# A host-planned linear-attention kernel: M's products spread over four pairs, its forms noted later, q's first loads given their own due times

## The chip, the core and the metric

The kernel runs on one core of a Trainium2 chip. The metric is the device time of one execution in microseconds; lower is better. Before the change the median of three runs is 572.95 us (572.63 to 574.16).

## The reference: what is computed

Two independent blocks A and B, each with its own x (2048 x 640), wqkv (640 x 1920) and wo (640 x 640), all in float32. 32 heads of 20 columns. The outputs stand side by side in the result (2048 x 1280).

```python
qkv = (x @ wqkv).reshape(B, S, 3, H, Dh).transpose(2, 0, 3, 1, 4)
q, k, v = qkv[0], qkv[1], qkv[2]
phi = lambda t: jnp.where(t > 0, t + 1, jnp.exp(t)) + 1e-6
pq, pk = phi(q), phi(k)
kv = jnp.einsum("bhsd,bhse->bhde", pk, v)
z = jnp.einsum("bhsd->bhd", pk)
num = jnp.einsum("bhqd,bhde->bhqe", pq, kv)
den = jnp.einsum("bhqd,bhd->bhq", pq, z)[..., None] + 1e-6
o = num / den
return o.transpose(0, 2, 1, 3).reshape(B, S, D) @ wo
```

## The kernel before

**What is computed in which order.** v is never formed. For each block the kernel first makes K = x wk, phi of it (pk), and G = pk' x (640 x 640, "gacc"). From G and wv come the 32 small matrices kv (in six groups of heads, GROUPS), and from those and wo one 640 x 640 matrix M; the output is then phi(q) / den times M. All products are float32 in three parts: each factor is split in a high part (rounded, made by ScalarE) and a low part (the rest, made by VectorE), and high x high, high x low and low x high are added in PSUM. K's products and the output products are done by Strassen-like schemes with seven products on 2 x 2 blocks ("forms" of the weight: sums of its blocks, each split in high and low).

**Stages.** K and G of block A, then K and G of block B, then q and the output of all eight 512-token units. In the K stage two token tiles of 128 make a pair; there are 16 pairs, p = 0 to 7 for A and 8 to 15 for B (NPB = 8). `kpair(p, fill)` writes the seven K products of a pair (banks 0, 1 and 2) and puts between them what `fill` names after step n: steps of G (`gstep`, 12 matmuls of 320 columns, banks 3 to 5), `kvmm(g, k)` (the kv of head group g, PSUM bank k), `mmm(g, k)` (the rows of M that belong to group g: load of wo, split, two products, copy, store of M's rows to DRAM). So A's kv and M are made while TensorE works on B's K. After the products of M come `zsums(0)` (the sums of phi(k) over the tokens, with one small store zd and four small gathers zq through DRAM) and `m_forms()`: M is read back from DRAM, its ten forms are made by VectorE (`forms`), split, and stored to DRAM by SyncE (`fd`), from where the output stage loads them. After B's last pair there are ten more steps of G, then q begins.

**What sets the order.** Up to the start of q nothing is written in the order in which an engine runs it. `note()` files a job (engine, cost, what it reads and writes), and `Plan.emit` simulates the engines on the host: at each moment an idle engine takes, of the jobs whose inputs are there and for which tiles are free, the one due first. TensorE's order is that of the calls. Due times run back from TensorE's ideal time: a job is due 0.2 us (LAG) before the first job that needs it, less its cost and, for a DMA, less 2.2 us and its transfer time. A job without followers is due `late` us (25, if not given) after TensorE's ideal time at the place where it was noted. `ahead` says how long before its due time a job may be taken at the earliest. `safe` lets the planner hold a job that needs a DMA's data for some us more, unless its due time comes first. A DMA is taken to be done 1.9 us after its transfer, and a tile is free for another use as soon as its last job is done in the simulation. On the chip each engine then runs its list in order and waits at semaphores: the list of SyncE (which issues most DMAs) stops at the first DMA that has to wait.

**Tiles.** Most data of the K stage lie in 42 tiles of 128 x 640: 4 "wo" (BO), 7 "wst" (BD) and 31 "gd" (GD); a job with `ANY` takes the first free one in this order. B's wv, six tiles that live on into the output stage, may lie in BD alone.

**The seam to q.** `swap` opens the tiles of q when the K stage's own are used up (`gate`). Then come, per 128 rows, the load of wq and its split (`high`, `low`), the load xqs of the first 512 columns of x' and its high part (`round`), the load xql of its low part from DRAM (`fetch`), and the six loads of wv; they are noted with `late` 25, the loads with `ahead` 20 and 30. From here on the order is the program's. q's first product needs wq and both parts of x' (L912 to L914); B's kv groups (L972, `kvmm2`) stand after q's steps (0,0), (0,3), (1,0), (1,3), (2,0) and (2,3) of unit 0 and use two PSUM banks in turn, which VectorE empties (L976). The last VectorE jobs of the plan are the end of B's z sums (L609 to L612), which wait for zq.

Of the kernel before, what the change touches and what calls it, by code (L numbers as in the profile page):

```python
# [15 lines left out]
DH = 20  # L16
EPS = 1e-6
GROUPS = [(0, 6), (6, 6), (12, 6), (18, 6), (24, 4), (28, 4)]
LAG = 0.2


class Space:
# [53 lines left out]
class Plan:  # L76
# [6 lines left out]
        self.jobs = []  # L83
        self.pe_at = 0.0

    def note(self, engine, n, fn, w, r, ahead=None, dma=None, late=None, by=None, due=None, safe=0.0):
        base = self.RATE.get(engine)
        j = Job(engine, base[0] + base[1] * n if base else n, fn, ahead, dma)
        for part, writes in [(p, True) for p in w] + [(p, False) for p in r]:
            sp = part.space  # L90
            if sp.where is not None and sp not in j.spaces:
                j.spaces.append(sp)
            for lo, hi, other, wrote in sp.uses:
                if lo < part.hi and part.lo < hi and (writes or wrote) and other is not j:
                    j.deps.add(other)
            if writes:
                sp.uses = [u for u in sp.uses if not (part.lo <= u[0] and u[1] <= part.hi and u[2] is not j)]
            sp.uses.append((part.lo, part.hi, j, writes))
        for d in j.deps:
            d.nexts.append(j)  # L100
        for sp in j.spaces:
            sp.left += 1
        if engine == "PE":
            j.ideal = self.pe_at
            self.pe_at += j.cost
        j.late = self.pe_at + (25.0 if late is None else late)
        if by is not None:
            j.late = self.pe_at + by
        j.by, j.set, j.safe = by, due, safe
        self.jobs.append(j)  # L110
        return j

    def emit(self, start, log=None):
        jobs = self.jobs
        for j in reversed(jobs):
            due = min([n.due - LAG for n in j.nexts], default=j.late)
            if j.by is not None:
                due = min(due, j.late)
            due -= j.cost + (2.2 + j.dma if j.dma else 0)
            if j.engine == "PE":  # L120
                due = min(due, j.ideal)
            j.due = due if j.set is None else j.set
# [14 lines left out]
        while n < len(jobs):  # L137
# [7 lines left out]
            for e in idle:  # L145
# [46 lines left out]
                queue[e].remove(best)  # L192
                if best.dma:
                    wire = max(wire, now) + best.dma
                    best.done = wire + 1.9
                    if e == "SP":
                        flying.append(best.done)
                    idle[e] = now + best.cost
                else:
                    best.done = idle[e] = now + best.cost  # L200
                events.update((idle[e], best.done, best.done + LAG))
                ends.append((best.done, best))
                best.fn()
                if log is not None:
                    log.append((now, e, best.fn.__code__.co_firstlineno, best, best.done))
# [10 lines left out]
def tile_linear_attn_pair(ctx: ExitStack, tc: tile.TileContext, ins, out: bass.AP):  # L216
# [79 lines left out]

    BK = [Bank("bank", k) for k in range(8)]

    def load(dst, src, n, ahead=14.0, due=None):
        note("SP", 0.07, lambda: nc.sync.dma_start(dst.f, src), [dst], [], ahead=ahead, dma=n * 512 / 330e3, due=due)  # L300

    def hi_of(hi, src, n):
        note("ACT", n, lambda: act(hi.r, src.f, AF.Copy), [hi], [src], ahead=10.0)
# [51 lines left out]
    def forms(kind, src, split, ready=()):  # L355

        f, raw = {}, {}
        for c in range(NC):
            raw[c] = t = Space(kind, D, ANY)
            note("SP", 0.07, lambda t=t, c=c: nc.sync.dma_start(t.all.f, src[c * P:(c + 1) * P, :]), [t.all],  # L360
                 [mdv[0:6]] if kind == "m" else [], ahead=14.0, dma=1.0)
        for k in range(2):
            m, n = raw[k], raw[2 + k]
            x, z = Space("t23", D, ANY), Space("t4", HF, ANY)
            note("DVE", HF, lambda m=m, n=n, x=x: tt(x[HF:D].f, n[HF:D].f, m[HF:D].f, op=OP.subtract),
                 [x[HF:D]], [n[HF:D], m[HF:D]], ahead=10.0)
            note("DVE", HF, lambda m=m: tt(m[HF:D].f, m[HF:D].f, m[0:HF].f, op=OP.subtract),
                 [m[HF:D]], [m.all], ahead=10.0)
            note("DVE", HF, lambda m=m, n=n, x=x: tt(x[0:HF].f, n[HF:D].f, m[HF:D].f, op=OP.subtract),
                 [x[0:HF]], [n[HF:D], m[HF:D]], ahead=10.0)  # L370
            note("DVE", HF, lambda n=n, x=x, z=z: tt(z.all.f, n[0:HF].f, x[0:HF].f, op=OP.subtract),
                 [z.all], [n[0:HF], x[0:HF]], ahead=10.0)
            f[k], f[2 + k], f[4 + k], f[6 + k] = m, x, n, z
        x, m = Space("d5", HF, ANY), raw[4]
        note("DVE", HF, lambda: tt(x.all.f, m[0:HF].f, m[HF:D].f, op=OP.subtract), [x.all], [m.all], ahead=10.0)
        f[8], f[9] = m, x
        out = dict(ready)
        for i in (0, 1, 2, 3, 4, 5, 8, 6, 7, 9):
            if i not in out:
                out[i] = split(i, f[i])  # L380
        return out
# [205 lines left out]
    def zsums(b):  # L587

        z, zt32 = Space("zsum", D, ANY), Space("zturn", D, ANY)
        for h in range(2):  # L590
            note("DVE", HF, lambda h=h: tt(z.all.f[:, h * HF:h * HF + HF], zac[b][h].all.f[:, :HF],
                                           zac[b][h].all.f[:, HF:], op=OP.add), [z[h * HF:h * HF + HF]], [zac[b][h].all], safe=6.0)
        part, four = Space("zpart", 20), Space("zfour", 20)
        pt, ft4 = zp[b]
        add = dict(axis=mybir.AxisListType.X, op=OP.add)
        note("DVE", D, lambda: nc.vector.transpose(zt32.all.f, z.all.f), [zt32.all], [z.all])
        note("DVE", D, lambda: nc.vector.tensor_reduce(
            pt.rearrange("p (g c) -> p c g", g=4), zt32.all.f.rearrange("p (c g t) -> p c g t", g=4, t=32), **add),
            [part.all], [zt32.all])
        zdv = Space("zd", 1)  # L600
        note("SP", 0.07, lambda: nc.sync.dma_start(zd[b], pt), [zdv.all], [part.all], dma=0.1)
        for g in range(4):
            note("SP", 0.07, lambda g=g: nc.sync.dma_start(
                ft4[g * 32:g * 32 + 32].rearrange("p (q c) -> p q c", q=4),
                zd[b].rearrange("(q i) (g c) -> g i q c", q=4, g=4)[g]), [four[g:g + 1]], [zdv.all], dma=0.1, safe=6.0)
        zt, s = zz[b]

        def finish():
            nc.vector.tensor_reduce(zt, ft4.rearrange("p (q c) -> p c q", q=4), **add)  # L609
            nc.vector.tensor_scalar(zt, zt, S * EPS, None, op0=OP.add)  # L610
            nc.vector.tensor_reduce(s, zt, **add)
            nc.vector.tensor_scalar(s, s, EPS, EPS / 4, op0=OP.mult, op1=OP.add)  # L612

        note("DVE", 300, finish, [KZ[b].all], [four.all], safe=6.0)
# [3 lines left out]
    def m_forms():  # L618
        def split(i, s):
            hi = Space("fsh", s.cols, ANY, F32R)  # L620
            lo = Space("fsl", s.cols, ANY, F32R)
            hi_of(hi.all, s.all, s.cols)
            lo_of(lo.all, s.all, hi.all, s.cols)
            fd[0, i] = [dram.tile([P, s.cols], F32, name=f"fd{t}0{i}") for t in "hl"]
            for d, t in zip(fd[0, i], (hi, lo)):
                note("SP", 0.07, lambda d=d, t=t: nc.sync.dma_start(d, t.all.f), [], [t.all], dma=s.cols / 640,
                     late=16.0 + 8.0 * (0, 2, 6, 4, 1, 3, 7, 5, 8, 9).index(i))

        forms("m", md[0], split)

# [161 lines left out]
    for c in range(NC):  # L792
        gstep(NG - 1, 0, c)
    wf[1] = forms("wk", ins[1]["wk"], w_split)
    kpair(NPB, filled(NG - 1, 1))
    kpair(NPB + 1, {0: [(kvmm, 0, 6)], 1: [(kvmm, 1, 7)], 2: [(kvmm, 2, 6)], 3: [(kvmm, 3, 7)],
                    4: [(kvmm, 4, 6), (kvmm, 5, 7)], 5: [(mmm, 0, 6)], 6: [(mmm, 1, 6)]})
    for p in range(NPB + 2, NP):
        i, h = divmod(p - NPB - 2, 2)
        gready(NG + i)  # L800
        fl = filled(NG + i, h, *((LAST,) if p == NP - 1 else ()))
        if p == NPB + 2:
            for n, g in ((0, 2), (2, 3), (4, 4), (6, 5)):
                fl.setdefault(n, []).append((mmm, g, 6))
        kpair(p, fl)
        if p == NPB + 2:
            zsums(0)
            m_forms()

    def swap():  # L810
# [28 lines left out]
    for c in range(NC):  # L839
# [8 lines left out]
            lo.make()  # L848
            tt(lo.all.r, raw.all.f, hi.all.f, op=OP.subtract)

        note("ACT", D, high, [hi.all], [raw.all, gate.all])
        note("DVE", D, low, [lo.all], [raw.all, hi.all])
        whl["q", 0, c] = hi, lo
    for c in range(NC):
        hi, lo, raw = late(q1b, "xqh", 512, 6), late(q1b, "xql", 512, 6), Space("xqs", 512, ANY)
# [7 lines left out]
            lo.make()  # L863
            nc.sync.dma_start(lo.all.f, xd[0][:, c].rearrange("p j s -> p (j s)"))

        note("ACT", 512, round, [hi.all], [raw.all, gate.all])
        note("SP", 0.07, fetch, [lo.all], [gate.all, xdv[0].all], ahead=30.0, dma=0.8)
        xt[0, c] = hi, lo
    for g, (h0, nh) in enumerate(GROUPS):
        cols = NC * DH * nh  # L870
        w = Space("wv", cols, (BD,))
        load(w.all, ins[1]["wv"][:, h0 * DH * NC:(h0 + nh) * DH * NC], cols, 30.0)
        w.left += 1
        wvt[1, g] = w
    plan.emit(1.0, globals().get("LOG"))
# [515 lines left out]
```

## Time and profile before

| | |
|---|---|
| median of three runs | 572.95 us (572.63 to 574.16) |
| the profiled execution | 574.53 us, of it the span of the instructions 572.8 us |
| TensorE busy | 565.7 us (99%), 3524 matmuls |
| VectorE, ScalarE, GpSimd busy | 434.3, 341.4, 57.2 us |
| DMA | 117.64 MB, mean 205 GB/s |
| granted TensorE clock | 0.999 |

In the rows below, PE is TensorE, PEld its loading of weights, DVE VectorE, ACT ScalarE, POOL GpSimd, SP SyncE; SPq is the issue of a DMA from SyncE's queue. A row of the timeline gives the start, the duration, engine, line, operation, out<-in, shapes and count, and in brackets the idle time before it and what ended it. Consecutive like instructions stand in one row. A row of the list of waits gives the total, the number and the longest. "DMA to landing" runs from issue to the end of the transfer. Times are in us from the start of the span.

### The profile page before, as it was taken

Reading aid. Unit: us, or ns where it says so; the run is one execution under the profiler, and the core shown is the slowest. Engines: PE = TensorE matmul, PEld = TensorE weight load, DVE = VectorE, ACT = ScalarE, POOL = GpSimd, SP = SyncE. Lnnn points to the kernel's source line nnn. Section 1 sums busy time; section 2 is a strip of 40 time slices with the busy share of each in tenths; the row PEclk is TensorE's granted clock in tenths of the full one; section 3 lists DMA queues with packets and bytes.
Section 4 is the critical chain, followed back from the end, with each engine's and each line's share of the span. In section 5 each row is a group of like instructions: output and inputs, shape, how many; then the busy total and the mean of one; then the engine's idle time right before and its main releaser. Section 6 shows DMA issues by size and latency. Waiting matters only on the chain.

```text
span 572.8 us, 9505 instructions
## 1 busy us (share of the span) xinstructions
PE 565.7 (99%) x3524; PEld 535.8 (94%) x3524; DVE 434.3 (76%) x706; ACT 341.4 (60%) x619; POOL 57.2 (10%) x93
## 2 busy tenths in 40 slices
PE   8999999999999999999999999999999999999997
PEld 6999999999999999999988899898989989898997
DVE  6788687599888589976555699967788786758792
ACT  6877566673786677655156665646556464644551
POOL 0210011110010011100000103120012201001010
PEclk9999999999999999999999999999999999999999
DMA  8994665758858889786787986663363996122022
GB/s 296 379 242 141 163 183 128 205 143 246 278 144 217 250 249 321 216 252 196 211 245 275 339 276 215 226 218 109 120 225 134 355 390 231 47 76 93 0 93 92
DMA packets 69441, 117.64 MB, mean 205 GB/s; under 512 B 7956, under 2 KB 31252, under 8 KB 69396
## 3 DMA queue, kind: packets, MB, share of 16 engines
q1 hardware_dynamic: 60500, 89.98, 48.2%
q0 software_dynamic: 8608, 26.88, 16.7%
q8 instruction: 27, 0.44, 0.3%
q10 hardware_dynamic: 288, 0.20, 0.1%
q14 instruction: 18, 0.15, 0.1%
HBM read 71.13 MB, written 35.41 MB: 186 GB/s over the span
## 4 chain that ended last, share of the span: by engine, by line
PE 89%; DMA 5%; DVE 3%; ACT 1%; issue 1%; SPq 1%; ACTq 0%; DVEq 0%
PE psg L312 20%; PE pa L1191 12%; PE ka L312 8%; PE psq L912 8%; PE psq L914 8%; PE psq L913 8%; PE pe L1191 6%; PE ke L312 4%; PE psk L711 4%; PE psb L1191 4%; PE kb L312 3%; DMA md<-mev 2%; DMA wk<-in_A_wk 1%; PE pskv L551 1%; PE pskv L972 1%; DMA xqs<-in_A_xt 1%
## 5 line engine op out<-in xcount | busy, mean ns | idle before, releaser
L312 PE MATMUL psg<-pkl,xnh 128*128 128x320 f32 x320 | 98.9, 309 | 0.0
L312 PE MATMUL psg<-pkh,xnh 128*128 128x320 f32 x320 | 98.8, 309 | 0.0
L312 PE MATMUL psg<-pkh,xnl 128*128 128x320 f32 x320 | 98.4, 308 | 0.0
L912 PE MATMUL psq<-xqh,wh 128*128 128x512 f32 x200 | 78.6, 393 | 1.0 <-ACT xqh L860 1.0
L914 PE MATMUL psq<-xqh,wl 128*128 128x512 f32 x200 | 78.0, 390 | 0.0
L913 PE MATMUL psq<-xql,wh 128*128 128x512 f32 x200 | 77.9, 390 | 0.0
L312 PEld LDWEIGHTS psg<-pkl,xnh 128*128 128x128 f32 x320 | 60.1, 188 | 0.0
L312 PEld LDWEIGHTS psg<-pkh,xnl 128*128 128x128 f32 x320 | 60.1, 188 | 0.0
L312 PEld LDWEIGHTS psg<-pkh,xnh 128*128 128x128 f32 x320 | 60.0, 188 | 0.0
L1206 ACT ACTIVATE o<-pa 128x320 f32<-128x320 f32 x64 | 27.9, 438 | 45.2 <-PE pa L1191 45.0
L484 ACT ACTIVATE kt<-ka 128x320 f32<-128x320 f32 x52 | 22.6, 435 | 52.2 <-PE ka L312 49.0
L1082 DVE SCALAR_TENSOR_TENSOR pq<-eq,rq 128x512 f32<-128x512 f32 x40 | 27.6, 691 | 30.7 <-ACT rq L1081 30.6
L401 POOL DMA_DIRECT2D zacc<-ek x32 | 26.4, 836 | 244.5 <-DVE ek L494 185.3
L532 DVE TENSOR_TENSOR gacc<-psg,gacc 128x320 f32<-128x320 f32 x60 | 29.4, 489 | 28.1 <-PE psg L312 27.3
L1080 ACT ACTIVATE eq<-psq 128x512 f32<-128x512 f32 x40 | 23.9, 597 | 36.6 <-PE psq L914 34.2
L912 PEld LDWEIGHTS psq<-xqh,wh 128*128 128x128 f32 x200 | 37.6, 188 | 8.5 <-ACT xqh L860 1.3
L914 PEld LDWEIGHTS psq<-xqh,wl 128*128 128x128 f32 x200 | 37.5, 188 | 7.9
L913 PEld LDWEIGHTS psq<-xql,wh 128*128 128x128 f32 x200 | 37.6, 188 | 7.2
L396 ACT ACTIVATE pkh<-ek,epst 128x640 fp32r<-128x640 f32 x32 | 26.5, 829 | 7.9 <-DVE ek L494 7.5
L1191 PE MATMUL pa<-fh,dah 128*128 128x320 f32 x96 | 29.7, 309 | 0.0
L1191 PE MATMUL pa<-fh,dal 128*128 128x320 f32 x96 | 29.7, 309 | 0.0
L1191 PE MATMUL pa<-fl,dah 128*128 128x320 f32 x96 | 29.7, 309 | 0.0
(213 smaller groups left out, 1553.3 us busy)
## 6 DMA issues: line engine op xcount, KB each, us to landing
zacc<-ek POOLq DMA_DIRECT2D x32, 320.0 KB, 5.8
xql<-xd SPq DMA_DIRECT2D x40, 256.0 KB, 5.9
xd<-xl SPq DMA_DIRECT2D x29, 320.0 KB, 6.2
out<-o POOLq DMA_DIRECT2D x28, 320.0 KB, 3.6
xns<-in_A_x SPq DMA_DIRECT2D x16, 320.0 KB, 5.8
xts<-in_B_xt_tiles SPq DMA_DIRECT2D x16, 320.0 KB, 4.3
xns<-in_B_x SPq DMA_DIRECT2D x16, 320.0 KB, 5.1
xqs<-in_A_xt SPq DMA_DIRECT2D x20, 256.0 KB, 6.0
```

Source lines behind the costliest of these rows:

```text
L312: nc.tensor.matmul(o, a.r, w.r, start=start and k == i == 0, stop=k == n - 1 and i == 2, skip_group_check=True)
L396: note("ACT", n + 110, lambda: act(hi.r, p.f, AF.Identity, bias=epst), [hi], [p, K0.all], by=8.0)
L401: note("POOL", 1.0, lambda: nc.gpsimd.dma_start(z.f, p.f, **kw), [z], [p], dma=1.0 if first else 1.86)
L532: tt(o, BK[k].tile[:, :HF], o, op=OP.add)
L711: nc.tensor.matmul(o[h][:, :HF], x[a].r, w[c][h * HF:h * HF + HF].r, start=c == 0 and i == 0, stop=c == NC - 1 and i == 2, skip_group_chec ...
L912: nc.tensor.matmul(o, whi, xhi, start=first, stop=False)
L913: nc.tensor.matmul(o, whi, xlo, start=False, stop=False)
L914: nc.tensor.matmul(o, wlo, xhi, start=False, stop=last)
L1080: nc.scalar.activation(e, ps, AF.Exp)
L1082: nc.vector.scalar_tensor_tensor(pq[u][:, c, :], e, 1.0, r, op0=OP.min, op1=OP.add)
L1191: nc.tensor.matmul(ps, x, y, start=start and n == i == 0, stop=n == len(terms) - 1 and i == 2, skip_group_check=True)
L1206: copy = lambda x, y: nc.scalar.activation(x, y, AF.Copy)
```

## The change

It changes, in the planner: a DMA is taken to be done 3.0 us after its transfer in place of 1.9 (loads of the start with a due time of their own keep 1.9), its due time allows for that, and a tile that a DMA reads or writes counts as free 6 us after the DMA. In the program: A's kv groups come three after step 1 and three after step 4 of pair 9; M's six products are put singly into pairs 9 to 12 (one, two, two, one); zsums(0) and m_forms() are noted after pair 12 in place of pair 10, with earlier `late` for the stores of the forms and `safe` 6 on the sums; zd and zq are issued by GpSimd in place of SyncE; q's first loads and splits get `late` and `ahead` of their own.

```diff
+LAT = 3.0
+REUSE = 6.0
...
-    def note(self, engine, n, fn, w, r, ahead=None, dma=None, late=None, by=None, due=None, safe=0.0):
+    def note(self, engine, n, fn, w, r, ahead=None, dma=None, late=None, by=None, due=None, safe=0.0, lat=0.0):
...
-        j.by, j.set, j.safe = by, due, safe
+        j.by, j.set, j.safe, j.lat = by, due, safe, (LAT if due is None else 1.9) + lat
...
-            due -= j.cost + (2.2 + j.dma if j.dma else 0)
+            due -= j.cost + (j.lat + 0.3 + j.dma if j.dma else 0)
...
-                    best.done = wire + 1.9
+                    best.done = wire + best.lat
...
-                events.update((idle[e], best.done, best.done + LAG))
-                ends.append((best.done, best))
+                free = best.done + (REUSE if best.dma else 0.0)
+                events.update((idle[e], best.done, best.done + LAG, free))
+                ends.append((free, best))
...
-    def load(dst, src, n, ahead=14.0, due=None):
-        note("SP", 0.07, lambda: nc.sync.dma_start(dst.f, src), [dst], [], ahead=ahead, dma=n * 512 / 330e3, due=due)
+    def load(dst, src, n, ahead=14.0, due=None, late=None):
+        note("SP", 0.07, lambda: nc.sync.dma_start(dst.f, src), [dst], [], ahead=ahead, dma=n * 512 / 330e3, due=due,
+             late=late)
...
     def forms(kind, src, split, ready=()):
 
         f, raw = {}, {}
+        safe = 6.0 if kind == "m" else 0.0
...
             note("DVE", HF, lambda m=m, n=n, x=x: tt(x[HF:D].f, n[HF:D].f, m[HF:D].f, op=OP.subtract),
-                 [x[HF:D]], [n[HF:D], m[HF:D]], ahead=10.0)
+                 [x[HF:D]], [n[HF:D], m[HF:D]], ahead=10.0, safe=safe)
...
-        note("SP", 0.07, lambda: nc.sync.dma_start(zd[b], pt), [zdv.all], [part.all], dma=0.1)
+        note("POOL", 1.0, lambda: nc.gpsimd.dma_start(zd[b], pt), [zdv.all], [part.all], dma=0.1, lat=2.0)
         for g in range(4):
-            note("SP", 0.07, lambda g=g: nc.sync.dma_start(
+            note("POOL", 1.0, lambda g=g: nc.gpsimd.dma_start(
...
-                     late=16.0 + 8.0 * (0, 2, 6, 4, 1, 3, 7, 5, 8, 9).index(i))
+                     late=10.0 + 6.5 * (0, 2, 6, 4, 1, 3, 7, 5, 8, 9).index(i))
...
-    kpair(NPB + 1, {0: [(kvmm, 0, 6)], 1: [(kvmm, 1, 7)], 2: [(kvmm, 2, 6)], 3: [(kvmm, 3, 7)],
-                    4: [(kvmm, 4, 6), (kvmm, 5, 7)], 5: [(mmm, 0, 6)], 6: [(mmm, 1, 6)]})
-    for p in range(NPB + 2, NP):
-        i, h = divmod(p - NPB - 2, 2)
-        gready(NG + i)
-        fl = filled(NG + i, h, *((LAST,) if p == NP - 1 else ()))
-        if p == NPB + 2:
-            for n, g in ((0, 2), (2, 3), (4, 4), (6, 5)):
-                fl.setdefault(n, []).append((mmm, g, 6))
+    place = ((1, 5, 0, 6), (2, 0, 1, 6), (2, 2, 2, 6), (3, 0, 3, 6), (3, 2, 4, 6), (4, 0, 5, 6))
+    kvs = {1: [(kvmm, g, (6, 7, 3)[g]) for g in range(3)], 4: [(kvmm, g, (4, 5, 6)[g - 3]) for g in range(3, 6)]}
+    for p in range(NPB + 1, NP):
+        if p == NPB + 1:
+            fl = kvs
+        else:
+            i, h = divmod(p - NPB - 2, 2)
+            gready(NG + i)
+            fl = filled(NG + i, h, *((LAST,) if p in (NPB + 2, NP - 1) else ()))
+        for q, n, g, k in place:
+            if q == p - NPB:
+                fl.setdefault(n, []).append((mmm, g, k))
         kpair(p, fl)
-        if p == NPB + 2:
+        if p == NPB + 4:
             zsums(0)
+        if p == NPB + 4:
             m_forms()
...
-        note("ACT", D, high, [hi.all], [raw.all, gate.all])
-        note("DVE", D, low, [lo.all], [raw.all, hi.all])
+        note("ACT", D, high, [hi.all], [raw.all, gate.all], ahead=15.0, late=9.0)
+        note("DVE", D, low, [lo.all], [raw.all, hi.all], ahead=15.0, late=9.0)
...
-        note("ACT", 512, round, [hi.all], [raw.all, gate.all])
-        note("SP", 0.07, fetch, [lo.all], [gate.all, xdv[0].all], ahead=30.0, dma=0.8)
+        note("ACT", 512, round, [hi.all], [raw.all, gate.all], late=9.5)
+        note("SP", 0.07, fetch, [lo.all], [gate.all, xdv[0].all], ahead=12.0, dma=0.8, late=8.0 + c)
...
-        load(w.all, ins[1]["wv"][:, h0 * DH * NC:(h0 + nh) * DH * NC], cols, 30.0)
+        load(w.all, ins[1]["wv"][:, h0 * DH * NC:(h0 + nh) * DH * NC], cols, 14.0, late=10.0 + 2 * g)
```

The other four sums of `forms` get `safe=safe` in the same way.

More of the change, by code (lines that the diff above doesn't have):

```diff
@@ L365, in forms @@
             note("DVE", HF, lambda m=m, n=n, x=x: tt(x[HF:D].f, n[HF:D].f, m[HF:D].f, op=OP.subtract),
-                 [x[HF:D]], [n[HF:D], m[HF:D]], ahead=10.0)
+                 [x[HF:D]], [n[HF:D], m[HF:D]], ahead=10.0, safe=safe)
             note("DVE", HF, lambda m=m: tt(m[HF:D].f, m[HF:D].f, m[0:HF].f, op=OP.subtract),
-                 [m[HF:D]], [m.all], ahead=10.0)
+                 [m[HF:D]], [m.all], ahead=10.0, safe=safe)
             note("DVE", HF, lambda m=m, n=n, x=x: tt(x[0:HF].f, n[HF:D].f, m[HF:D].f, op=OP.subtract),
-                 [x[0:HF]], [n[HF:D], m[HF:D]], ahead=10.0)
+                 [x[0:HF]], [n[HF:D], m[HF:D]], ahead=10.0, safe=safe)
             note("DVE", HF, lambda n=n, x=x, z=z: tt(z.all.f, n[0:HF].f, x[0:HF].f, op=OP.subtract),
-                 [z.all], [n[0:HF], x[0:HF]], ahead=10.0)
+                 [z.all], [n[0:HF], x[0:HF]], ahead=10.0, safe=safe)
             f[k], f[2 + k], f[4 + k], f[6 + k] = m, x, n, z
         x, m = Space("d5", HF, ANY), raw[4]
-        note("DVE", HF, lambda: tt(x.all.f, m[0:HF].f, m[HF:D].f, op=OP.subtract), [x.all], [m.all], ahead=10.0)
+        note("DVE", HF, lambda: tt(x.all.f, m[0:HF].f, m[HF:D].f, op=OP.subtract), [x.all], [m.all], ahead=10.0, safe=safe)
         f[8], f[9] = m, x
```

## The prediction

> **What bounds the kernel now.** I read the page first, then the list of who waited for whom on TensorE, then the timeline of TensorE around each wait, and last the timelines of SyncE, ScalarE and VectorE behind it.
>
> ```profile
> span 572.8 us, 9505 instructions
> ## 1 busy us (share of the span) xinstructions
> PE 565.7 (99%) x3524; PEld 535.8 (94%) x3524; DVE 434.3 (76%) x706; ACT 341.4 (60%) x619; POOL 57.2 (10%) x93
> ```
> ```profile
> PE psq L912 <- ACT xqh L860: 1.0, 1, 1.0
> PE psi L639 <- DVE ones L320: 1.0, 1, 1.0
> PE ke L312 <- DVE kt L488: 0.7, 1, 0.7
> PE psk L711 <- ACT wkh L303: 0.5, 1, 0.5
> PE ka L312 <- ACT kt L484: 0.2, 1, 0.2
> ```
> TensorE is the bound: 565.7 of 572.8 us. The change adds and removes no matmul, so all that it can gain is in the waits. Two of the five (psi, psk) lie in the first microseconds, whose loads have a due time written by hand and keep their latency of 1.9; I leave them as they are. Three are left. What they cost is read from the starts of the matmuls, since the list shows only the gap after the pipeline has drained:
>
> ```profile
> 179.31 0.31 PE L578 MATMUL psm<-woh,kvl 80*80 80x320 f32 x1
> 179.87 0.42 PE L312 MATMUL ka<-wkh,xh 128*128 128x320 f32 x1 [0.25 <-ACT kt L484]
> ```
> ```profile
> 204.71 0.31 PE L312 MATMUL ka<-wkh,xl 128*128 128x320 f32 x1
> 205.74 0.41 PE L312 MATMUL ke<-wkh,xsh 128*128 128x320 f32 x1 [0.71 <-DVE kt L488]
> 205.99 0.31 PE L312 MATMUL ke<-wkl,xsh 128*128 128x320 f32 x1
> 206.14 0.31 PE L312 MATMUL ke<-wkh,xsl 128*128 128x320 f32 x1
> ```
> ```profile
> 289.29 0.31 PE L312 MATMUL psg<-pkh,xnl 128*128 128x320 f32 x1
> 290.61 0.50 PE L912 MATMUL psq<-xqh,wh 128*128 128x512 f32 x1 [1.02 <-ACT xqh L860]
> ```
> Two matmuls of 320 columns follow each other every 0.15 us (205.99 to 206.14). The three pairs above are 0.56, 1.03 and 1.32 us apart, so 0.41, 0.88 and 1.17 are lost, and the step after a wait takes 0.25 in place of 0.15 (205.74 to 205.99), 0.10 more each: 0.51, 0.98 and 1.27, in sum **2.76 us**. That is the most these three can give back. The list of weight loads has a second, short wait for L488 beside the one at 205.74:
>
> ```profile
> PEld ke L312 <- DVE kt L488: 1.2, 2, 1.0
> ```
> Its 0.2 I don't count, but it belongs to the lower end of the range.
>
> **The change part by part.** The program's order on each engine comes from a planner on the host; an engine then runs its list in order and waits where it must. So the change is one of order alone, and its price is which wait comes last where.
>
> *Planner's constants (latency 1.9 to 3.0 us, 6 us before a tile is reused that a DMA touched).* Two waits behind the first stall:
>
> ```profile
> 174.22 0.44 ACT L484 ACTIVATE kt<-ka 128x320 f32<-128x320 f32 x1 [2.18 <-DMA zacc<-ek]
> ```
> ScalarE stood 2.18 us, since the tile it was to write was still being read by the accumulating DMA. With 6 us kept free after a DMA the planner hands it another tile. It was this lost time that made ScalarE's copy too late for the matmul at 179.87; I count the 0.51 as gained. The price is tiles held longer. What hides it is that loads are asked for 12 to 16 us ahead of their due time (`ahead` in the code), so that one which gets its tile 6 us later still lands in time: nothing, and up to 0.51 (the same stall elsewhere) if that cover is gone.
>
> *M's products over four pairs, its forms later, `safe` = 6 on their sums.* Behind the second stall:
>
> ```profile
> 187.93 6.29 DMA md<-mev
> ```
> ```profile
> 194.35 3.24 DMA m<-md
> ```
> ```profile
> 198.59 0.49 DVE L365 TENSOR_TENSOR t<-m 128x320 f32<-128x320 f32 x1 [3.71 <-issue]
> ```
> M's last rows left at 187.93 and took 6.29 us to DRAM, where the planner assumed 1.9 + 1.0; SyncE stood until then, read M back at 194.35 (3.24 us), and VectorE, whose next instruction was the first sum of the forms, stood 3.71 us. From there it was late until the matmul at 205.74. In the new order the last product of M is at the head of pair 12 and the forms are noted at that pair's end, about 16 us after it (a pair has 54 matmuls of K and 60 of G, 114 by 0.147 = 16.8 us); the sums are asked for at least 6 us after the planned landing where their due time allows. The planner's error (6.29 + 3.24 against 4.0 + 4.0 now) is 1.5 us, less than those 6. I count 0.98 as gained. What is late next is VectorE's load, since the forms' sums and splits move some 20 us back (from two pairs, less what their due times gain):
>
> ```profile
> 210.00:250.00 40.00, 40.00 (x275) 40.00 (x274) 36.41 (x67) 25.66 (x43) 3.42 (x4) 1.00 0.89 265
> 250.00:270.00 20.00, 20.00 (x139) 20.00 (x138) 12.98 (x22) 12.34 (x21) 2.58 (x3) 1.00 0.74 218
> ```
> VectorE (the fourth figure) is busy 36.41 of 40 us up to 250 and 12.98 of 20 after it, so they go where there is room. The form stores move along in SyncE's list, the last of them in between q's loads; each holds the queue until its split is done.
>
> *q's first loads.* In the order of before:
>
> ```profile
> 263.21 1.83 SPq L300 DMA_DIRECT2D wv<-in_B_wv  x4
> 267.63 2.23 SPq L864 DMA_DIRECT2D xql<-xd  x5
> 269.91 0.90 SPq L300 DMA_DIRECT2D wv<-in_B_wv  x2
> 275.47 8.44 SPq L300 DMA_DIRECT2D wq<-in_A_wq  x5
> 284.01 0.38 SPq L601 DMA_DIRECT2D zd<-zp  x1
> 284.43 5.02 SPq L300 DMA_DIRECT2D xqs<-in_A_xt  x5
> 289.54 1.80 SPq L603 DMA_DIRECT2D zq<-zd  x4
> ```
> ```profile
> 289.93 2.57 ACT L860 ACTIVATE xqh<-xqs 128x512 fp32r<-128x512 f32 x4 [1.49 <-DMA xqs<-in_A_xt]
> ```
> What q wants first (wq, xqs) goes last, behind wv, whose six groups are wanted one by one from 0.8 us after q's first matmul on. By the code, a wq load was due at 25 - 0.82 - 0.2 - 0.72 - 0.2 - 3.26 = 19.8 us after the planned end of G, and with ahead = 20 it was open from 0.2 before it; now it is due at 9 - 1.94 - 4.36 = 2.7 and open from 17.3 before. An xqs load moves from 1.1 after the end to 15.5 before. So both go to the front, where SyncE now takes wv and xql (263 to 270). They still need free tiles: the last pair's last accumulation is issued at 271.84 (row below), so I put the last free tile near 272. If the five wq start there, and take as now 8.44 us, xqs goes out from about 280.5, and five of them as now in 5.02 us; the first lands, by its row,
>
> ```profile
> DMA to landing us min/median/max: 5.7/6.4/7.0
> ```
> at 286.9, and ScalarE needs 0.64 for it: 287.5. q then begins at 290.61 - 2.76 = 287.85. That is the late end, with no tile free before 272; I count the 1.27 as gained.
>
> *zd and zq go from SyncE to POOL.* Five small DMAs leave SyncE's queue and pass none of its loads any more; on POOL nothing is queued behind them but the two accumulations per pair. Who waits is VectorE: the end of the z sums (L609) stands in its list ahead of q's first mask product (L976), which frees the PSUM bank that the third pskv group takes.
>
> ```profile
> 271.84 0.85 POOL L401 DMA_DIRECT2D zacc<-ek  x1 [2.27 <-DVE ek L494]
> ```
> ```profile
> 283.00 0.81 DVE L597 TENSOR_REDUCE zp<-zturn 128x20 f32<-128x640 f32 x1
> ```
> ```profile
> DMA to landing us min/median/max: 2.9/4.1/6.8
> ```
> ```profile
> 293.60 0.19 DVE L609 TENSOR_REDUCE z<-zq 128x5 f32<-128x20 f32 x1 [1.16 <-DMA zq<-zd]
> ```
> ```profile
> 294.29 0.27 DVE L976 TENSOR_TENSOR kvt<-pskv,mask 120x120 f32<-120x120 f32 x1
> ```
> ```profile
> 297.00 1.21 PE L972 MATMUL pskv<-gacc,wv 128*120 128x120 f32 x10
> ```
> The sums end at 283.81. In the new clock that is 283.81 - 1.49 (the two stalls ahead of it) + 1.1 (the accumulation is planned to land later) = 283.4. One store landing and one gather landing (row of these tiles: 2.9 to 6.8, median 4.1; I take 4.1 and the shorter 2.9 that an empty queue gives), and three POOL issues of 0.85 between: 283.4 + 2.9 to 4.1, + 2.55, + 2.9 to 4.1 = 291.8 to 294.2. From L609 to the end of L976 it is about 1.0 us: 292.8 to 295.2. The third group wants the bank at 297.00 - 2.76 = 294.24. So it is hidden by 1.4 us or late by 1.0; with 6.8 for each landing it would be late by 6.3. I take 0.2, near the short end, because POOL's queue is empty there.
>
> The Trainium skill, *SBUF — State Buffer*, section "SBUF: two separate sides", speaks against this part: a DMA issued from GpSimd can have its descriptors starved while VectorE runs an operation that uses both read ports, 3.1 us for one that takes 0.62 alone. The trace does not agree for this kernel's operations: with VectorE 76% busy the issue above took 0.85 us. By the rule this part would cost what the second rival below does, or more.
>
> *The new order as a whole* also moves work that has no stall today (33 to 160 us). For that I add one small wait of the size of the gap at 179.87, 0.3.
>
> **Sum.** -0.51 - 0.98 - 1.27 + 0.2 + 0.3 = **-2.26 us**. The profiled execution took 574.53 us (span 572.8), 1.58 above the median of the runs, 572.95; it would become 572.3, and the median **570.7 us**. About 0.3% (1.72 us) is what a measurement of this kernel can tell from no change: the boundary is 571.23.
>
> **The rivals.** *Half of it:* the middle stalls go but q's start stays late, because the loads wait for tiles whatever their place in the list. For it: wq's five loads took 8.44 us to issue, which is waiting, not issuing. Against it: they now stand ahead of xql and wv. Then 572.95 - 1.49 + 0.3 = 571.8.
>
> *The gathers from POOL arrive late,* because each issue there waits for the VectorE operation that runs (0.81 for the one at 283.00): five issues make 4.05, L976 ends at 294.0 + 4.05 = 298.05 against 294.24, and the time is 570.5 + 3.8 = 574.3; with one landing of 6.8 alone (2.7 more than 4.1) it is 570.5 + 2.5 = 573.0. For it: no row shows a small DMA from POOL. Against it: the 0.85. By the figures of that page of the Trainium skill, 2.5 us more for each, it would be an estimated 583.
>
> *Slower: wv loses its head start.*
> ```profile
> 288.28 1.55 DVE L849 TENSOR_TENSOR wl<-wq,wh 128x640 fp32r<-128x640 f32 x2
> ```
> ```profile
> 291.42 1.21 PE L972 MATMUL pskv<-gacc,wv 128*120 128x120 f32 x10
> ```
> wv may lie only in seven tiles, six of which it keeps; wq and xqs, now ahead of it, take from the same ones. If wv gets its tile only when VectorE has split wq (first one done 0.8 after 288.28, in the new clock 287.6), it lands 6.4 later, at 294.0, and the first pskv, wanted at 291.42 - 2.76 = 288.66, waits 5.3 us: 570.7 + 5.3 = 576.0. The kernel is slower than before once that landing passes 290.9 (288.66 + 2.25). Against it: the splits are due 16 us sooner than they were (9 in place of 25) and open from 7.7 us before the planned end of G, so that the tiles come free earlier than 287.6.
>
> *Nothing changes:* the waits only move to other places of the same size, 572.95 within 0.5.
>
> **How the numbers follow.** Forecast 0.58 (its own range 569.5 to 571.2: from all 2.76 gained, with a second short wait of the same kind and the 0.3 by which the runs differ, to 1.0 lost again); half of it 0.15 (571.2 to 572.2); late gathers 0.09 (571.0 to 574.3); wv late 0.09 (572 to 576.0); nothing 0.09. From 569.5 to 573.2 lies a little over 0.8 of this; the upper ends of the two slow cases are left out. Faster: 0.58 + 0.03 of the half case + 0.01 of the gathers = 0.62. Slower: 0.03 of the gathers + 0.07 of wv = 0.10. Same, the rest: 0.28.
>
> **What would show it.** Right: TensorE's list of waits has no line for xqh L860, and those for kt L484 and L488 are gone or below 0.3; SyncE issues wq and xqs ahead of wv, from before 272; VectorE has no wait of 3.7 at L365; zq lands before 294 and L976 does not make pskv wait. The forecast is wrong if TensorE shows a new wait at pskv L972 (on wv or on L976), if xqh stays in the list, or if the matmuls of 33 to 160 us show gaps that they don't have now.

## The result and the profile after

Before: 572.79 us median of 6 runs (571.95 to 576.57). After: 580.52 us of 6 (579.57 to 581.08). The ratio is 1.0122, 95% interval 1.0093 to 1.0151: slower, where 570.7 was forecast. The profiled execution of after took 581.08 us (span 579.3).

The page of after, first lines, and TensorE's list of waits (us in total, times, longest):

```profile
span 579.3 us, 9490 instructions
...
PE 567.1 (98%) x3524; PEld 537.5 (93%) x3524; DVE 434.3 (75%) x706; ACT 341.4 (59%) x619; POOL 63.1 (11%) x103
```
```profile
PE pskv L981 <- DVE kvt L985: 6.3, 1, 6.3
PE psi L644 <- DVE ones L324: 1.0, 1, 1.0
PE psk L716 <- ACT wkh L307: 0.7, 1, 0.7
PE pskv L981 <- DVE gacc L537: 0.7, 1, 0.7
```

All three stalls of before (kt twice, xqh) are gone, as forecast. In their place stands one of 6.3 us, at the third pskv group of q, and a short one at the first. The matmuls around the long one, TensorE's timeline (start, duration, line, what, wait before it):

```profile
291.33 0.39 PE L922 MATMUL psq<-xql,wh 128*128 128x512 f32 x1
291.55 0.39 PE L923 MATMUL psq<-xqh,wl 128*128 128x512 f32 x1
...
292.47 1.21 PE L981 MATMUL pskv<-gacc,wv 128*120 128x120 f32 x10
293.44 0.48 PE L921 MATMUL psq<-xqh,wh 128*128 128x512 f32 x1
...
294.68 0.40 PE L923 MATMUL psq<-xqh,wl 128*128 128x512 f32 x1
301.42 2.36 PE L981 MATMUL pskv<-gacc,wv 128*120 128x120 f32 x10 [6.34 <-DVE kvt L985]
303.44 0.77 PE L921 MATMUL psq<-xqh,wh 128*128 128x512 f32 x1
...
304.87 0.63 PE L921 MATMUL psq<-xqh,wh 128*128 128x512 f32 x1
305.30 0.63 PE L922 MATMUL psq<-xql,wh 128*128 128x512 f32 x1
...
306.02 0.40 PE L921 MATMUL psq<-xqh,wh 128*128 128x512 f32 x1
```

A psq follows the one before it after 0.22 to 0.23 us (291.33 to 291.55), so 294.68 to 301.42 loses 6.74 - 0.23 = 6.51. (The short one at the first group, read the same way, loses about 0.8.) After it the engine is slow for a while: 0.43 from one psq to the next (304.87 to 305.30), and the pskv group takes 2.02 to the next start (301.42 to 303.44) where the one before took 0.97. The granted clock (PEclk, the third figure from the end) says the same: in the stretch 301.42 to 306.02 it is 0.52, against 1.00 ahead of the wait.

```profile
core 0: us, PE busy (x) PEld busy (x) DVE busy (x) ACT busy (x) POOL busy (x), PEclk, DMA share, GB/s
301.42:306.02 4.60, 4.60 (x17) 4.07 (x18) 2.02 (x6) 3.11 (x7) 0.00 (x0) 0.52 0.19 42
291.10:292.47 1.37, 1.37 (x8) 1.12 (x6) 0.00 (x0) 0.00 (x0) 0.00 (x0) 1.00 0.96 274
```

That is another 2.02 - 0.97 = 1.05, and 2.58 - 1.47 = 1.11 on the six psq behind it (303.44 to 306.02; the same six took 293.44 to 294.68 plus 0.23). So 6.5 of wait and 2.2 of slow clock. The Trainium skill, *TensorE: Matmul & The Clock Gate*, section "Part 1: The HAM clock gate", says that about 3.4 us of idling halve the clock until about as much time busy has passed. The trace agrees: 6.34 us idle, then 0.52 for 4.6 us.

Who is late is read from the chain of waits, backwards from 301.42 (start, length, what):

```profile
286.67 0.41 DVE zsum L596
...
287.98 0.83 DVE zp L602
...
289.10 7.25 DMA zd<-zp
...
296.64 1.67 POOL zq L608 x3
298.31 2.01 DMA zq<-zd
...
300.40 0.20 DVE z L614
...
301.18 0.20 DVE kvt L985
...
301.42 2.36 PE pskv L981 x10
```

Two things are seen here. The sums of z come later: zp ends at 288.81 (before: 283.81). And the 10 KB store zd, forecast at 2.9 to 4.1, takes 7.25. VectorE stands 11.2 us at L614, and kvt, which needs nothing of z, is behind it in its list. SyncE's timeline shows what is under way meanwhile:

```profile
264.83 3.24 SPq L303 DMA_DIRECT2D wq<-in_A_wq  x5
268.12 2.43 SPq L303 DMA_DIRECT2D xqs<-in_A_xt  x3
...
282.25 2.23 SPq L303 DMA_DIRECT2D wv<-in_B_wv  x5
287.05 2.62 SPq L971 DMA_DIRECT2D wo<-in_B_wo  x6
289.71 4.33 SPq L952 DMA_DIRECT2D xqs<-in_A_xt  x3
```

wq and xqs are ahead of wv, as wanted. But the loads for q's next stage, wo and xqs, also go out at 287.05 and 289.71. In before they went out at 291.85 and 294.56, behind zq, which stood in SyncE's own list with zd. But SyncE did not stand there for either: zd went out at 284.01, 0.1 us behind the last wq, and zq at 289.54, behind five xqs. What kept SyncE busy so long in before were q's own loads, which had to wait for tiles (in its list of waits, 3.8 us for zturn and 2.8 for wl). In after these loads are all out by 284.48, zd and zq are no longer in the list, and wo waits only for a matmul of G (2.5 us).

### The profile page after: what moved, and what is told of

It reads as the page before. It is cut to its first block, busy times and chain, and to the rows that moved or that the text cites. A ratio compares the mean times of both kernels' runs of the same rounds, so it can differ in the third digit from the quotient of the medians.

```text
span 579.3 us, 9490 instructions
## 1 busy us (share of the span) xinstructions
PE 567.1 (98%) x3524; PEld 537.5 (93%) x3524; DVE 434.3 (75%) x706; ACT 341.4 (59%) x619; POOL 63.1 (11%) x103
## 4 chain that ended last, share of the span: by engine, by line
PE 95%; DMA 3%; DVE 1%; POOL 0%; SPq 0%; issue 0%; ACT 0%; DVEq 0%
PE psg L316 24%; PE pa L1200 12%; PE ka L316 10%; PE psq L921 8%; PE psq L922 8%; PE psq L923 8%; PE pe L1200 6%; PE ke L316 5%; PE psk L716 4%; PE psb L1200 4%; PE kb L316 3%; DMA zd<-zp 1%; DMA wk<-in_A_wk 1%; PE pskv L556 1%; PE psm L583 1%; PE pskv L981 1%
```

## The experiments

Four kernels first, against two theories. "Place": the sums of z come later and their end stands ahead of kvt in VectorE's list, and that is the harm, whoever issues zd and zq. "POOL": the harm is the move of zd and zq to POOL. All ratios are to runs of the kernel before that were made beside them.

**e1, zd and zq of B back on SyncE.**
```diff
+        eng, cost, by = ("SP", 0.07, nc.sync) if b else ("POOL", 1.0, nc.gpsimd)
-        note("POOL", 1.0, lambda: nc.gpsimd.dma_start(zd[b], pt), ..., dma=0.1, lat=2.0)
+        note(eng, cost, lambda: by.dma_start(zd[b], pt), ..., dma=0.1, lat=0.0 if b else 2.0)
```


> The changed kernel with B's zd and zq issued by SyncE again (A's stay on POOL). Theory 'place': in the changed kernel VectorE comes to B's second z sum only at 286.58 (281.24 before), since the planner lists it behind the splits of wq; the end of the sums, which waits for zq, stands ahead of the product that frees a PSUM bank, and who issues the small DMAs matters little. Then the sums still end near 288.8, zq lands near 298, the third pskv still waits 3 to 6 us, and the time is 576 to 580. Rival 'POOL': the small DMAs are late because GpSimd issues them. Then zq lands before 294, the wait is gone, and the time is 570 to 571.5.

572.03 us, ratio 0.9975 (0.9963 to 0.9988). "Place" is refuted: zp ends as late as in after (288.41), and yet the long wait is gone. Its timeline:

```profile
288.44 0.33 SPq L607 DMA_DIRECT2D zd<-zp  x1
289.87 1.76 SPq L609 DMA_DIRECT2D zq<-zd  x4
291.73 2.64 SPq L972 DMA_DIRECT2D wo<-in_B_wo  x6
293.06 0.19 DVE L615 TENSOR_REDUCE z<-zq 128x5 f32<-128x20 f32 x1 [4.25 <-DMA zq<-zd]
```

zd has landed 1.43 us after its issue, a zq takes 1.7 (median of the four), and wo goes out behind them: in this order SyncE does stand, 4.2 us for zp and 1.0 for zd's landing. From zp's end to L615 it is 4.65 us; in after 11.60.

**e2, the sums of B asked for sooner, POOL kept.**
```diff
-            ... [zac[b][h].all], safe=6.0)
+            ... [zac[b][h].all], safe=0.0 if b else 6.0)
-        note("DVE", 300, finish, [KZ[b].all], [four.all], safe=6.0)
+        note("DVE", 300, finish, [KZ[b].all], [four.all], safe=6.0, late=0.0 if b else None)
```


> The changed kernel with B's z sums planned sooner (no 6 us of safety after the accumulation, and a due time 25 us earlier); the small DMAs stay on POOL. Theory 'place': VectorE's sums end near 283.7 instead of 288.8, zq lands near 295, the wait at the third pskv is 0 to 1.5 us, and the time is 569.5 to 572.5. Rival 'POOL': the landing and the four issues of GpSimd stay as long as they are and TensorE still waits 4 us or more: 576 or above.

578.88 us, ratio 1.0092 (1.0064 to 1.0121). zd goes out at 283.41, 5.7 us sooner, and the wait for kvt is still 4.0: zd's landing holds zq back until 288.72, and zq, now among wo and xqs, is there at 297.1. So earlier sums alone don't mend it. In this run zp ends at 283.11, where the forecast had it (283.4), and the two landings take 5.03 us for zd and 6.66 for the last zq, with the DMA engines fully taken during both (share 1.0 or a little over); the forecast counted 2.9 to 4.1 for each.

**e3, the end of B's z sums put at a step of q, POOL kept.**
```diff
-        note("DVE", 300, finish, [KZ[b].all], [four.all], safe=6.0)
+        if b:
+            ends[b] = finish
+        else:
+            note("DVE", 300, finish, [KZ[b].all], [four.all], safe=6.0)
...
+    at(("q", 1, 0, 0), ends[1])
```


> The changed kernel with only the end of B's z sums (four small VectorE operations that wait for zq and are first needed in unit 4) moved out of the plan to q's step (1,0,0). Both theories: the late zq blocks nobody, the 6.3 us and the slow matmuls behind them are gone, and all that the change gained shows: 569.5 to 571, with the 0.7 us wait of the first pskv for the last addition of G still there. Rival: another wait takes its place (the sums are not the only thing late), 573 or above.

571.92 us, ratio 0.9978 (0.9964 to 0.9992). zd is as slow as in after (issued 288.12, POOL waits 7.05 for it), but nobody waits behind it. So the late zq costs time only through VectorE's list.

**e4, q's due times as before, POOL kept** (wl, xqh and xql likewise).
```diff
-        note("ACT", D, high, [hi.all], [raw.all, gate.all], ahead=15.0, late=9.0)
+        note("ACT", D, high, [hi.all], [raw.all, gate.all])
...
-        load(w.all, ins[1]["wv"][...], cols, 14.0, late=10.0 + 2 * g)
+        load(w.all, ins[1]["wv"][...], cols, 30.0)
```

> The changed kernel with the due times and `ahead` of q's first loads and splits as before (the middle stage, the planner's constants and the small DMAs on POOL stay changed). Theory 'place': the z sums are back ahead of the splits, the long wait is gone or below 1 us, q's start waits for xqh again (about 1.3), and the time is 570.8 to 572.5. Rival 'POOL': zq stays late by 3 us or more and the time is 575 or above.

576.57 us, ratio 1.0050 (1.0032 to 1.0068), not the 570.8 to 572.5 of "place". zp ends early again (283.28), and zd and zq are slow again, but the wait that counts is another: psq for xqh, 3.6 us. The "575 or above" of "POOL" came true, but not by its path.

The four runs leave a third theory, "held queue". Its first half: a 10 KB transfer is slow when bulk loads are under way, whoever issues it. Its second half: in before, SyncE's stop for zd kept that bulk back. e5, e6 and e9 test it.

**e5, after with SyncE held until zq has landed; zd and zq stay on POOL.**
```diff
+        if b:
+            zh = dram.tile([P, 20], F32, name="zh")
+            note("SP", 0.07, lambda: nc.sync.dma_start(zh, ft4), [], [four.all], dma=0.1)
```


> After, and one small store more on SyncE, of B alone: it reads the turned-back sums, so SyncE stands from its place until zq has landed. zd and zq stay on POOL. Theory 'held queue' (in before, SyncE stopping for zd's data and landing kept the loads of the next unit off the DMA engines; after lets them through, and the five 10 KB transfers land among them): wo and xqs go out only behind zq, zd lands in 1.4 to 3 us and not in 7.25, the wait of the third pskv group for kvt falls from 6.3 to under 1, 570.5 to 572.5. Theory 'POOL' (the transfers are slow because POOL issues them, whatever else is under way): zd still takes 5 us or more, the wait stays at 4 or more, 577 or more.

574.2 us, ratio 1.0009 (0.9994 to 1.0023). The chain shows zd from POOL at 1.73 us:

```profile
288.16 1.73 DMA zd<-zp
...
290.18 1.67 POOL zq L608 x3
291.85 1.91 DMA zq<-zd
```

The wait for kvt is 0.7 and the clock stays at 1.00. This is the theory's mechanism, but its time is 1.7 above the range given: its span is 1.5 above e1's, and two places make that up, 0.89 at the third pskv group (by 293.74 to 294.86 in TensorE's timeline) and 0.66 at 315.92, where xql is late since SyncE let everything go 2.5 us later than in e1. From zp's end (287.86) to the first operation of z's end (293.84) it is 5.98 against e1's 4.65: POOL itself costs 1.3 of the 6.95 us by which after is behind e1, the bulk the rest.

**e6, before with only B's zd and zq on POOL.**
```diff
+        eng, cost, by = ("POOL", 1.0, nc.gpsimd) if b else ("SP", 0.07, nc.sync)
```


> Before, with B's zd and zq moved to POOL and nothing else. Theory 'held queue': the sums come as early as in before (zp about 283 to 284), but SyncE doesn't stop any more and zd takes 4 to 7 us among the loads; the third pskv group waits 0 to 3 us, and xqh's wait stays at 1 or grows; 573 to 577. Rival 'the move does harm only with the sums late': zq lands before the third group is due, no wait for kvt, 572.5 to 573.5. Were POOL slow by itself, the wait would be 3 or more and the time 576 or more.

573.8 us, ratio 1.0003 (0.9986 to 1.0020): no difference. zd takes 5.61 us here too (POOL waits 5.32 behind its issue), beside q's five xqs loads, but the sums come early enough (zp ends at 285.45) and wo goes out only at 293.91. The time lies in the range of "held queue" too, but the wait for kvt that it allowed did not come: the rival read it better. And the theory's second half falls: without zd and zq in its list SyncE sends wo no sooner than before's 291.85 (here wo waits 5.2 us for an xqs), so in before's order their place held nothing back. It does so in e1's order. The move does its harm where the next bulk is early: with early sums (e2) the wait is 4.0, with late sums and the bulk held (e5) 0.7, and with both against it (after) 6.3.

**e9, e1 with bulk put ahead of zd on SyncE; no POOL.**
```diff
+        def out():
+            if b:
+                zh = dram.tile([P, 20], F32, name="zh")
+                nc.sync.dma_start(zh, pt)
+                for k in range(6):
+                    zk = dram.tile([P, 533], F32, name=f"zk{k}")
+                    nc.sync.dma_start(zk, ins[1]["wv"][:, k * 533:k * 533 + 533])
+            by.dma_start(zd[b], pt)
```


> e1 (B's zd and zq on SyncE, the order of everything else as it was there), with extra work on SyncE right ahead of zd: one 10 KB store of zp, which makes SyncE wait for it, and then six copies of 273 KB each from one place in device memory to another, 1.6 MB that nobody reads. POOL has no part in it. Theory 'held queue' (what makes a 10 KB transfer slow is the bulk that is on its way, whoever issues it): zd goes out about 2.7 us later and lands after 5 us or more, not 1.4; zq goes out behind that; the third pskv group waits 4 to 9 us for kvt, the granted clock falls behind it, 576 to 582. Theory 'SyncE's transfers are quick by themselves': zd lands within 2.5 us, the wait is the 2.7 us of the later start and no more, 573 to 575.

581.82 us, ratio 1.0145 (1.0115 to 1.0174): after's loss, made without POOL. Its chain and its wait:

```profile
287.87 0.33 SPq L611
...
292.14 5.22 DMA zd<-zp
...
297.38 0.33 SPq L619
```
```profile
PE pskv L992 <- DVE kvt L996: 7.3, 1, 7.3
```

The later start is 4.3 us, not 2.7 (the copies took 0.59 to 0.64 each to issue), and zd's landing 5.22 in place of 1.43. So about half of the loss is the later start, and 3.8 the bulk. Beside each other, the stretch from zd's issue to its landing in five kernels (length, then the engines, granted clock, DMA share, GB/s), e1 (SyncE), e5 (POOL), e9 (SyncE), after (POOL) and before (SyncE):

```profile
288.44:289.87 1.43, 1.00 (x9) 1.01 (x10) 0.37 (x1) 0.00 (x0) 0.00 (x0) 1.00 0.07 8
```
```profile
288.16:289.89 1.73, 1.58 (x12) 1.54 (x13) 0.10 (x1) 0.00 (x0) 0.57 (x1) 1.00 0.04 6
```
```profile
292.14:297.36 5.22, 2.00 (x12) 1.38 (x10) 0.00 (x0) 0.00 (x0) 0.00 (x0) 0.91 0.66 189
```
```profile
289.10:296.35 7.25, 5.83 (x35) 4.84 (x35) 0.10 (x1) 0.00 (x0) 0.57 (x1) 1.00 1.00 286
```
```profile
284.01:287.84 3.83, 3.83 (x29) 3.83 (x28) 0.98 (x2) 1.62 (x3) 0.00 (x0) 1.00 0.94 281
```

The landing is short from either queue when the share of DMA time that is taken is small (0.07, 0.04), and long from either when it is large (0.66, 0.94, 1.00). The share alone doesn't set the length: before's own zd landed in 3.83 at 0.94, and A's zd, from SyncE in the same execution, took 6.82 at 1.01. Whether a transfer from POOL's queue fares worse at the same share isn't shown; A's zd of e12 took 8.95 from SyncE at 0.85, longer than any from POOL. VectorE is busy 0.10 us in after's 7.25 and POOL's issue took 0.57, so it isn't POOL waiting for VectorE either.

**e8, the middle alone:** e1 and e4 together. Left of the change are M's products and forms, the planner's constants and margins, and A's zd and zq on POOL.
```diff
 the edits of e1 and of e4
```

> After, with q's first loads as in before and B's zd and zq on SyncE as in before: M's products over four pairs, the forms a pair sooner and the planner's constants are what is left. Theory 'the gains add up as in the sum': the two waits of the middle (0.51 and 0.98) are gone and xqh's of 1.0 to 1.3 stays, 571.5 to 572.8. Rival 'the middle is worth nothing by itself': the same as before, 573.0 to 573.6.

576.36 us, ratio 1.0054 (1.0033 to 1.0074): both were wrong. The middle's waits are gone, but xqh's is 3.2 us, after which the clock falls as well (0.83 over 290 to 300):

```profile
PE psq L922 <- ACT xqh L870: 3.2, 1, 3.2
```
SyncE sends wq only at 280.13 here, behind all six wv (before: 275.47, behind them too). The same wait stands in e4, at 3.6. With the rest of the change in place, q's old due times are worse than they were in before; which part of it does that is not shown.

**e10, q's order alone:** e1 with the middle as in before. Constants, margins and A's zd and zq on POOL are kept.
```diff
+    kpair(NPB + 1, {0: [(kvmm, 0, 6)], 1: [(kvmm, 1, 7)], 2: [(kvmm, 2, 6)], 3: [(kvmm, 3, 7)],
+                    4: [(kvmm, 4, 6), (kvmm, 5, 7)], 5: [(mmm, 0, 6)], 6: [(mmm, 1, 6)]})
...
-                     late=10.0 + 6.5 * (0, 2, 6, 4, 1, 3, 7, 5, 8, 9).index(i))
+                     late=16.0 + 8.0 * (0, 2, 6, 4, 1, 3, 7, 5, 8, 9).index(i))
...
-        if p == NPB + 4:
+        if p == NPB + 2:
             zsums(0)
```

> After with the middle as in before: M's products and forms stand where they stood, their stores' due times too; B's zd and zq on SyncE as in before; what is left of the change is the order of q's first loads, and the planner's constants with the additions' margins. Where the parts add up: xqh's wait of 1.0 is gone, the middle's two waits of 0.5 and 1.0 stay, 572 to 573. Where the planner's constants bring the harm that was seen with q's loads as before (a time above 575): 575 or more here too.

571.8 us, ratio 0.9976 (0.9956 to 0.9995). xqh's wait is gone, and so are the middle's two, though M's products and forms stand where they stood. e1, which differs from it by these alone, has 0.9975: spreading M over four pairs is worth nothing that these runs can tell.

**e12, before with q's due times and nothing else** (e4's lines the other way round, in before).
```diff
-        note("ACT", D, high, [hi.all], [raw.all, gate.all])
+        note("ACT", D, high, [hi.all], [raw.all, gate.all], ahead=15.0, late=9.0)
...
-        load(w.all, ins[1]["wv"][...], cols, 30.0)
+        load(w.all, ins[1]["wv"][...], cols, 14.0, late=10.0 + 2 * g)
```

> Before, with q's due times of the change and nothing else: the middle, the planner's constants, the margins and SyncE for zd and zq all as in before. Theory 'the gain is q's order': xqh's wait is gone, the middle's waits of 0.5 and 0.7 to 1.0 are left, 571.8 to 572.6 beside before's 573. Theory 'the planner's constants took the middle's stalls' predicts the same waits, and a time some 0.5 to 1.4 above e10's 571.8, thus 572.3 to 573.2. If z's sums come later here too (zp at 287 or so), it is q's earlier splits on VectorE that do it, since all else is as before.

574.67 us, ratio 1.0018 (1.0000 to 1.0036), above all that was expected. xqh's wait is gone, but the middle's are there, larger in this execution than in before's, and a new one of 0.7 came:

```profile
PE ke L312 <- DVE kt L488: 2.3, 2, 1.6
...
PE pskv L972 <- DVE gacc L532: 0.7, 1, 0.7
PE ka L312 <- ACT kt L484: 0.4, 1, 0.4
```
zp ends at 291.48 here, 7.7 us later than in before, of which the larger stalls of this execution explain about 2; the rest is q's order. e10 has the same middle without these stalls: what took them is among the constants, the margins and A's zd and zq on POOL.

**e7, e3 with G's last additions ahead of zp, and e11, e7 with zd and zq on SyncE.**
```diff
-        note("DVE" if g else "ACT", HF, keep, [go], [BK[k].all])
+        note("DVE" if g else "ACT", HF, keep, [go], [BK[k].all], late=0.5 if i == LG else None)
```
e11 adds e1's edit to this.

> e3 (the end of B's z sums stands in VectorE's order at a step of q, not ahead of kvt), with G's last additions ahead of zp in VectorE's order. What e3 left was one wait of 0.7 of the first pskv group for an addition into G. If that wait is all that is to be had there, it goes and the time is 0.5 to 0.9 below e3's 571.9: 571.0 to 571.4. If the wait is only shifted (zp later, z later, or the group waits for a bank), 571.7 to 572.2.

> e7 (the end of B's z sums at a step of q, G's last additions first) with B's zd and zq on SyncE. If z's end is off TensorE's path in e7, nothing is left to gain by it: 571.0 to 571.8, as e7's 571.4, and TensorE waits for no z, psq or pskv. If SyncE's stop for zd holds wo and xqs back too long: 572 or more.

571.4 us, ratio 0.9965 (0.9952 to 0.9977), and 571.09 us, ratio 0.9965 (0.9951 to 0.9979). Both are below before and after, with intervals clear of 1. e11's list of waits holds one line, in the first microseconds:

```profile
PE psi L650 <- DVE ones L324: 1.0, 1, 1.0
```
With z's end off VectorE's path to kvt, these two runs show no difference by who issues zd and zq, though in e7 zd again took over 6 us.

## Why the prediction was wrong, point by point

- **The step that failed: zd and zq on POOL, "0.2, near the short end, because POOL's queue is empty there".** It measured 6.5 us of waiting and 2.2 of slow clock. POOL's queue was empty, the DMA engines were not. The step kept before's landings and read the shorter one, 2.9, as that of an empty queue; but zd's 3.8 and zq's 2.9 in before had come with a DMA share of 0.94 and 0.64. And it didn't ask what would keep wo and xqs back once q's loads were out early and SyncE had no zd to wait for: two parts of the change that are harmless apart (e6 has the one, e1 the other) and cost this together. e2 is the clean case, with the sums where the forecast had them: landings of 5.0 and 6.7, and a wait of 4.0. e1 against after is the price of this part: 0.9975 to 1.0122. That the step's own outer bound, 6.3 us late with 6.8 for each landing, is near the 6.5 is luck: after is made up of late sums, one landing of 7.25 and one of 2.0.
- **"The sums end at 283.4".** 288.81. The +1.1 was for a later planned landing; what q's new order does to VectorE's list was left out. Seen in e1, e10 and e12 (288 to 291.5), and gone in e4 and e8, where q has its old order. In the forecast's own sum these 5.4 us alone make the group late by 3.9 to 6.3 (288.8 + 2.9 to 4.1 + 2.55 + 2.9 to 4.1 + 1.0 against 294.24). In e1 they didn't, since zd and zq together took 4.65 there and not the 8.4 to 10.8 of the sum. What is left of them in e1 is about the 0.7 at the first pskv group (e7 takes that away).
- **The clock behind a long wait** wasn't priced: 2.2 us, part of the step above.
- **The rival "the gathers from POOL arrive late"** had the place (z's end ahead of kvt), with another cause, issues that wait for VectorE, and 573.0 to 574.3. B's five issues took 0.55 to 0.59 each, with VectorE nearly idle, and the cause is bulk.
- **The two stalls of the middle, 0.51 and 0.98:** gone, as forecast, but M's new places weren't needed for it (e10): something else in the change suffices.
- **xqh, 1.27:** gone, by q's order, as forecast: wq goes out at 264.83, sooner than the 272 taken for the late end. The rival that wv loses its head start didn't come: TensorE waits for wv in no run.
- **The sum of gains, 2.76,** was mis-sized against the median. It was read from an execution of 574.53 us; the span of e11 is 3.7 below that one's 572.8, but its ratio to the runs of before, which spread from 571.5 to 576.4, is 0.9965, 2.0 us. Stalls of this kind differ from one execution to the next: by starts, the middle's are 1.3 in the profile of before (0.41 + 0.88), 2.7 in e6's and 3.2 in e12's, whose middles have the same code. One profile's sum isn't the median's. The 0.3 for work that moves between 33 and 160 us isn't seen: in after no two matmuls there start more than 0.45 us apart.
- **Left open:** which of the constants, the margins and A's move to POOL takes the middle's stalls, and why VectorE's second zsum comes behind G's last additions. In the code the planner books all transfers on one wire, and q's ten loads now stand there; that this is the reason is argued, not shown.

## What to carry to other kernels

A transfer that an engine stops for also holds back all that is queued behind it. Before such a transfer is moved to another queue, ask which bulk loads are then free to go, and ask it of the changed order: in before's order the move was free, in the new one it cost some 8 us. Price a small transfer by what will be under way where it travels, not by the depth of its own queue, and where bulk is under way try the sum with the longest landing on record. And put what waits for a late transfer behind the instructions that free the bound engine's buffers: e3 made the lateness free by moving one note.

## What the runs showed of the hardware

A 10 KB store took 1.41 to 1.73 us to land with the DMA engines nearly idle (shares of 0.04 to 0.07, in e10, e1 and e5), and much longer with 0.85 or more of their time taken: from SyncE's queue 3.83 and 6.82 (before, B's and A's) and 8.95 (e12, A's), from POOL's 4.73 (e4), 5.03 (e2), 5.61 (e6), 7.25 (after) and 7.34 (e3). The Trainium skill, *DMA: Bandwidth & Descriptors*, section "Queues, rings and completion order", has the engines take turns between queues packet by packet. By that, one would expect a small transfer on POOL's queue to pass the bulk of SyncE's soon; after's 7.25 us, in which 286 GB/s moved, don't show that.
